# Windowed attention and an MoE-like mixer on one core: batch 0's score tiles and input, its mixing units in three banks, and a table of task ranks

## The chip, the cores and the metric

The kernel runs on one core of a Trainium2 chip, all eight batches one after the other. The metric is the device time of one execution in microseconds (us). The engines are PE (matrix products), PEld (PE's weight loads), DVE, ACT and POOL (elementwise work), and SP, on whose queue this kernel issues its loads and stores. Each engine works through its own instructions in the order in which the program lists them.

## The reference

```python
B, H, S, D = 8, 8, 576, 64
scores = q @ k.transpose(0, 1, 3, 2) / sqrt(D)
rel = pos[:, None] - pos[None, :]
mask_plain = (rel >= 0) & (rel < 32)                        # heads 0 to 3
mask_dil = (rel >= 0) & (rel < 128) & (rel % 4 == 0)        # heads 4 to 7
attn = softmax(where(mask, scores, -1e9))
x = (attn @ v).transpose(0, 2, 1, 3).reshape(B, S, 512)
theta = x @ w_theta                                         # 512 x 512
zr, zi = x * cos(theta), x * sin(theta)
y = einsum('ts,bsd->btd', w_tok_r, zr) + einsum('ts,bsd->btd', w_tok_i, zi)
u = x + y                                                   # w_tok: 576 x 576 each
out = u + relu(u @ w_ch)                                    # 512 x 512
```

q, k and v are float32; the weights arrive as 64-bit floats.

## The kernel before

**Attention.** Two heads make a pair, four pairs a batch. The sequence of a dilated head is permuted so that its window is 32 wide as well. A pair's 576 queries are 18 blocks of 32, and a block needs 64 keys. In `scores` one matmul serves one block of both heads: the queries stand as the 128 x 64 weight tile (two heads of 64 dims, and 64 columns, 32 for each head), with zeros where row and column belong to different heads, so that one product gives both heads' 32 rows of 64 scores. Two blocks fill the 128 partitions of one strip, nine strips a pair, in two PSUM banks of the pool `s`: strips 0 to 4 (20 PE instructions with the weight loads, as the trace counts them) and 5 to 8 (16). In batch 0 the mask is added by PE too (`mask_on_pe`): a matmul of the identity `ids` with the mask `mskb` opens each bank, and the scores add to it. Then come the maximum and the exponentials (line 626, three strips of 64 keys on ACT for each of the names P_0 to P_3), transposes, and `pv`, which gives x.

**Mixing.** All products of batch 0 behind theta are three products of split numbers: a high part (a cast to fp32r, `high`, line 455 on DVE or 458 on ACT) and a low part (the rest, `low`, line 463 on DVE or 466 on POOL). `theta0` makes theta of batch 0 for five tiles of the sequence (the last has 64 rows), `trig` its cosine and sine products, the nine tiles `z_0` to `z_8` with their low parts. A **unit** is one PSUM bank's worth of the work behind it: eight token units (`token`: 128 of the 512 features by half of the 576 positions, nine steps of three matmuls, 27 in all, one step for each z tile, in the order KORD), then eight channel units (`chan`, line 1453: four steps of three matmuls, one for each u tile). The first four token units use the first half of the token weights (`wt_g`, `wtkh`, `wtkl`), the other four the second half, `late_wt_a` and `late_wt_b`; the channel units use `late_wc`. These late tiles take the room of tiles of the attention of batch 0 and of the first weights.

**Weights.** `unpack` turns the 64-bit floats into float32: a load into a staging tile `st_...`, a clamp on DVE, an ACT step, a shift on DVE or ACT (the table SHIFT), and a merge on DVE (line 447); then the cast and the low part, each on an engine that small tables of keys choose (HIS, LOS, XLO, XEV, ZHI, ZLO, UHI, ULO). EARLY, LATE and LATE2 name the staging tiles; each load waits until its staging tile is free.

**The order.** `Order` is a list scheduler that runs while the program is built. Every part of the work is a generator that yields an engine and a cost in ns ahead of its instructions, or an event to wait for. Of the tasks that are ready on an engine it takes the one of lowest rank and writes its instructions down; the engines then run them in that order, and the tiles' semaphores keep the data right. RANK holds a number for each family of tasks; to it the program adds a step for each member (.01, or `pair` = 0.36 for the attention). All of batch 0, the attention and theta of batch 1 and the start of batch 2's scores are ordered in this way. From batch 1's first token unit on a planner with due times takes over (`steady`), one batch in 61.4 us.

The units of batch 0 are one task, one unit after the other, each in one of the two banks `m`:

```python
    def units(b):
        for f, i, g in UNITS:
            yield from f(b, i, g)
...
    go(units(0), RANK["units"])
```

and the scores, line 588 on, with `mask_on_pe` ahead of them:

```python
                for e in range(2):
                    qb = 2 * n + e
                    pe(nc.tensor.matmul(ps[64 * e:64 * e + 64, n - g0], q[:, qb],
                                        k[:, QB * qb:QB * qb + BW], start=not masked, stop=not masked or n == g1 - 1))
```

The functions that the change touches:

## Time and profile before

| | |
|---|---|
| three runs | 558.38, 558.6, 561.25 us; median 558.6 |
| profiled execution | 557.5 us, of which the span is 555.6 |
| mean granted PE clock | 0.991 |
| DMA | 124.42 MB, mean 224 GB/s |
| chain that ended last, by engine | PE 73%, ACT 8%, DMA 6%, DVE 5%, POOL 4% |

The span reaches from the first to the last instruction of the profiled execution; 1.9 us of it lie outside the span. Busy shares, windows and the rows of single stretches stand in the prediction. In those rows the columns are the start in us from the span's start, the duration, the engine, line, operation, the names `out<-in`, and how many instructions were merged (`x20`); brackets at the end give the engine's idle time ahead of it and what ended that. `128*64 128x64` on PE is a weight tile of 128 rows and 64 columns, and a result or operand of 128 x 64. A row of grouped instructions gives the busy time in us and the mean of one in ns. In a window's row stand PE, PEld, DVE, ACT and POOL busy, with the number of instructions in brackets, then the granted PE clock, the DMA engines' share, and GB/s.

### The profile page before, as it was taken

Reading aid. Unit: us, or ns where it says so; the run is one execution under the profiler, and the core shown is the slowest. Engines: PE = TensorE matmul, PEld = TensorE weight load, DVE = VectorE, ACT = ScalarE, POOL = GpSimd, SP = SyncE. Lnnn points to the kernel's source line nnn. Section 1 sums busy time; section 2 is a strip of 40 time slices with the busy share of each in tenths; the row PEclk is TensorE's granted clock in tenths of the full one; section 3 lists DMA queues with packets and bytes.
Section 4 is the critical chain, followed back from the end, with each engine's and each line's share of the span. In section 5 each row is a group of like instructions: output and inputs, shape, how many; then the busy total and the mean of one; then the engine's idle time right before and its main releaser. Section 6 shows DMA issues by size and latency. Waiting matters only on the chain.

```text
span 555.6 us, 14351 instructions
## 1 busy us (share of the span) xinstructions
PE 531.7 (96%) x5296; PEld 481.5 (87%) x5296; DVE 435.8 (78%) x1354; ACT 374.3 (67%) x1032; POOL 330.8 (60%) x349
## 2 busy tenths in 40 slices
PE   4899798999999999999999999999999999999997
PEld 3744687887898899998999899989999899989997
DVE  2878897995589697989799997989799988848422
ACT  1489977759938578668776777768775777467320
POOL 1227968799983274664477385656468365717660
PEclk9999799999999999999999999999999999999999
DMA  8993445644289947995489918994699826690722
GB/s 291 401 357 109 152 124 180 231 142 146 83 278 300 312 187 268 334 295 199 148 315 329 324 64 266 361 272 156 205 331 287 293 86 218 206 271 32 234 86 86
DMA packets 59127, 124.42 MB, mean 224 GB/s; under 512 B 5424, under 2 KB 24624, under 8 KB 58800
## 3 DMA queue, kind: packets, MB, share of 16 engines
q1 hardware_dynamic: 59056, 123.49, 64.9%
q8 instruction: 42, 0.69, 0.5%
q14 instruction: 29, 0.24, 0.1%
HBM read 99.88 MB, written 23.59 MB: 222 GB/s over the span
## 4 chain that ended last, share of the span: by engine, by line
PE 73%; ACT 8%; DMA 6%; DVE 5%; POOL 4%; issue 2%; SPq 0%; POOLq 0%; DVEq 0%; ACTq 0%
PE c L1453 15%; PE th L819 12%; PE C L1212 9%; PE D L1212 7%; PE A L1212 7%; PE o L750 6%; PE B L1212 4%; PE y L1420 4%; PE s L591 4%; DVE pt L650 2%; PE th L801 2%; DMA va<-in_vw_dram 2%; DMA st_wtk<-in_wtk_dram 1%; DMA q<-in_qT_dram 1%; ACT P L626 1%
## 5 line engine op out<-in xcount | busy, mean ns | idle before, releaser
L650 DVE STREAM_TRANSPOSE pt<-P 32x288 f32<-32x288 f32 x224 | 105.1, 469 | 11.3 <-POOL P L632 7.0
L1453 PE MATMUL c<-u,late_wc 128*128 128x288 f32 x768 | 109.1, 296 | 0.4 <-POOL late_wc L466 0.2
L1453 PEld LDWEIGHTS c<-u,late_wc 128*128 128x128 f32 x768 | 105.5, 188 | 4.0 <-DVE x L1429 0.7
L626 ACT ACTIVATE P<-P,mx 128x64 f32<-128x64 f32 x252 | 84.4, 337 | 3.0 <-DVE mx L530 2.9
L819 PE MATMUL th<-wthh,xh 128*128 128x512 f32 x224 | 75.0, 395 | 0.6 <-DVE K L1354 0.6
L632 POOL TENSOR_TENSOR P<-P,mx 128x576 f32<-128x576 f32 x32 | 38.7, 1210 | 59.9 <-DVE mx L630 51.6
L530 DVE CUSTOM_DVE_ANT_0 P<-s,mskb 128x64 f32<-128x64 f32 x252 | 39.0, 218 | 19.7 <-PE s L591 19.5
L1228 ACT CAST u<-x 128x288 fp32r<-128x288 f32 x48 | 20.6, 430 | 45.3 <-DVE x L1238 44.8
L819 PEld LDWEIGHTS th<-wthh,xh 128*128 128x128 f32 x224 | 42.0, 188 | 10.2 <-DVE K L1354 1.1
L1230 POOL TENSOR_TENSOR u<-x,u 128x288 fp32r<-128x288 f32 x48 | 41.7, 875 | 14.4 <-ACT u L1228 14.0
L626 ACT ACTIVATION_READ_ACCUMULATOR P<-P,mx 128x1 f32 x252 | 47.2, 187 | 0.0
L819 PE MATMUL th<-wthl,xh 128*128 128x512 f32 x112 | 44.4, 396 | 0.0
L710 ACT COPY x<-o 128x576 f32<-128x576 f32 x32 | 29.5, 921 | 20.0 <-PE o L750 20.0
L466 POOL TENSOR_TENSOR zl<-g,zh 128x512 fp32r<-128x512 f32 x7 | 9.1, 1299 | 49.3 <-ACT zh L458 49.3
L591 PE MATMUL s<-k,q 128*64 128x64 f32 x1008 | 37.0, 227 | 1.1 <-DVE K L1354 0.9
L591 PEld LDWEIGHTS s<-k,q 128*64 128x64 f32 x1008 | 33.1, 141 | 4.9 <-issue 2.3
L1429 DVE SCALAR_TENSOR_TENSOR x<-c,x 128x288 f32<-128x288 f32 x64 | 28.3, 449 | 11.6 <-PE c L1453 11.4
L750 PEld LDWEIGHTS o<-pt,va 128*64 128x64 f32 x600 | 20.3, 137 | 10.8 <-DVE pt L650 3.6
L750 PE MATMUL o<-pt,va 128*64 128x64 f32 x600 | 24.7, 227 | 4.9 <-DVE pt L650 3.3
L992 POOL TENSOR_TENSOR s<-f,x 128x256 f32<-128x256 f32 x24 | 17.8, 743 | 11.9 <-DVE f L980 9.7
L819 PEld LDWEIGHTS th<-wthl,xh 128*128 128x128 f32 x112 | 21.0, 188 | 4.1
L1420 PE MATMUL y<-wt_g,z 128*128 128x288 f32 x96 | 21.3, 327 | 3.4 <-POOL z L466 2.3
(245 smaller groups left out, 1583.7 us busy)
## 6 DMA issues: line engine op xcount, KB each, us to landing
q<-in_qT_dram SPq DMA_DIRECT2D x32, 576.0 KB, 5.5
late_wt_a<-tw_t SPq DMA_DIRECT2D x24, 576.0 KB, 6.2
wt_g<-tw_b SPq DMA_DIRECT2D x22, 576.0 KB, 6.4
va<-in_vw_dram SPq DMA_DIRECT2D x30, 320.0 KB, 5.2
k<-in_kT_dram SPq DMA_DIRECT2D x28, 304.0 KB, 5.6
out_dram<-x SPq DMA_DIRECT2D x28, 288.0 KB, 2.1
vb<-in_vw_dram SPq DMA_DIRECT2D x29, 256.0 KB, 4.3
xd<-xq SPq DMA_DIRECT2D x24, 288.0 KB, 4.9
```

Source lines behind the costliest of these rows:

```text
L530: pin(nc.vector.tensor_tensor_reduce(out=P[:, n], in0=ps[:, n - g0], in1=mskb[:, mask_of(pr, n)], op0=ALU.add, op1=ALU.min, scale=-SCALE, ...
L591: pe(nc.tensor.matmul(ps[64 * e:64 * e + 64, n - g0], q[:, qb], k[:, QB * qb:QB * qb + BW], start=not masked, stop=not masked or n == g1 - 1))
L626: table(nc.scalar.activation(P[:, n], P[:, n], AF.Exp, bias=mx[:, n:n + 1], scale=-1.0, accum_out=sm[:, n, :1]))
L632: pin(nc.gpsimd.tensor_tensor(P, P, mx.unsqueeze(2).to_broadcast([128, NJ, BW]), op=ALU.mult))
L650: pin(nc.vector.transpose(pmats[b, pr][k0:k0 + QB, :, hh, QB * e:QB * e + QB], P[p0:p0 + QB, :, QB * o:QB * o + QB]))
L710: pin(nc.scalar.copy(dst, src))
L750: pe(nc.tensor.matmul(ps[64 * hh:64 * hh + 64, BW * j:BW * j + BW], v[:, 64 * hh:64 * hh + 64], pmats[b, pr][:, j, hh], start=True, stop=T ...
L819: pe(nc.tensor.matmul(pt, l, r, start=(n == 0), stop=(n == 3 * NC - 1)))
L1212: pe(nc.tensor.matmul(ps, l, r, start=first and n == 1, stop=last and n == 3 * len(ks), skip_group_check=more))
L1230: pin(nc.gpsimd.tensor_tensor(ul[b, d][:, ts], x[:, ts], uh[b, d][:, ts].bitcast(F32), op=ALU.subtract))
L1420: pe(nc.tensor.matmul(ps, l[:, cs], r, start=(n == 0), stop=(n == 3 * NK - 1)))
L1453: pe(nc.tensor.matmul(ps, l[:, cs], r[:, ts], start=(n == 0), stop=(n == 3 * NC - 1)))
```

## The change

It has four parts.

1. **Scores of batch 0.** Its queries come as an input of their own, `q0`, without the zeros: 128 x 576 for a pair, 288 KB in place of 576 KB. A block of 32 queries is two matmuls now, one for each head, with 64 rows and 32 columns of weights, so a pair has 72 of the PE instructions where it had 36. They open the bank, and the mask is added behind them and closes it. The loads of the mask and the identity move behind the queries and keys of the first pair on SP's queue. Batches 1 to 7 keep their form.
2. **Units of batch 0.** Each of the 16 units is a task with a rank. Unit n waits for the end of unit n - 3 (LANES), so three are open at a time; U0 gives them banks of the pools t, x and s as well as m, and token units go through the z tiles in the order KORD0.
3. **Ranks.** RANK has a number for each task: each pair, each weight tile, each theta tile, each unit. Turns (the flips of batch 1 and 2), evacuations and the trig work of each theta tile have their own.
4. **Engines and rooms.** The tables that choose DVE, ACT or POOL for casts, low parts and shifts are different, the staging tiles EARLY, the banks of theta and x in batch 1 (TP1, XN1), and two delays (AT1 12 to 10, SLACK 500 to 0).

The diff, cut:

```diff
-EARLY = ('u0', 'u1', 'u2', 'u3', 'xh0')
+EARLY = ('xh2', 'u2', 'u1', 'u3', 'xh1')
...
-RANK = dict(load=6.64, scores0=1.09, flip=0.01, pv0=1.13, pair=0.36, theta_unpack=1.54, theta0=5.3, trig0=2.031, token_early=4.156, theta_split=6.42, token_late=5.835, chan=2.1, units=2.95, evacuate=4.49, scores1=4.02, scores2=7.3, pv1=8.0, theta1=5.96, trig1=8.298)
-SHIFT = (('wth', 0), ('wth', 2), ('wtk0_', 0), ('wtk0_', 2), ('wtk0_', 4))
+RANK = dict(
...
+    units=(1.534, 1.575, 1.534, 1.534, 1.534, 1.534, 1.534, 4.786, 4.642, 6.706, 1.534, 4.702, 4.682, 4.692, 4.672, 4.712),
...
+SHIFT = (('wth', 0), ('wth', 2), ('wth', 3), ('wtk0_', 2), ('wtk0_', 4))
...
-LOS = ()
-XLO = (0, 1, 2)
-XEV = ()
-ZHI = ((0, 8),)
-ZLO = ((1, 6),)
-UHI = ((1, 2, 0),)
-ULO = ((1, 3, 0),)
+LOS = (('wch', 3), ('wth', 1), ('wtk', 1, 4))
+XLO = (2,)
+XEV = ((0, 3),)
+ZHI = ((0, 8), (1, 0), (1, 2), (1, 4))
+ZLO = ((1, 1), (1, 3))
+UHI = ((1, 1, 0), (1, 2, 0), (1, 2, 1), (1, 3, 0), (1, 3, 1))
+ULO = ((0, 1, 1), (1, 0, 0), (1, 0, 1), (1, 2, 1), (1, 3, 1))
...
+KORD0 = (0, 4, 1, 5, 7, 2, 6, 8, 3)
+LANES = 3
...
-TP1 = {4: 't', 0: 't', 1: 't', 2: 't', 3: 't'}
+TP1 = {4: 't', 0: 't', 1: 't', 2: 's', 3: 'x'}
...
-XN1 = {4: 'x', 0: 's', 1: 'x', 2: 'm', 3: 'x'}
+XN1 = {4: 's', 0: 's', 1: 's', 2: 'm', 3: 'x'}
...
-U0 = 'mmmmmmmmmmmmmmmm'
+U0 = 'mmtmmtmmxmmmmsmm'
...
     def first_loads():
-        yield "DMA", dma(3 * BW + 64)
-        pin(nc.sync.dma_start(mskb, maskb.bitcast(BF16)))
-        pin(nc.sync.dma_start(idb, identb.bitcast(BF16)))
         for pr in range(NP):
...
-            yield "DMA", dma(2 * S)
-            pin(nc.sync.dma_start(q, qT[0, pr]))
+            yield "DMA", dma(S)
+            pin(nc.sync.dma_start(q, q0[pr]))
...
             if pr == 0:
+                yield "DMA", dma(3 * BW + 64)
+                pin(nc.sync.dma_start(mskb, maskb.bitcast(BF16)))
+                pin(nc.sync.dma_start(idb, identb.bitcast(BF16)))
...
-                                start=(n == g0), stop=False))
+                                start=False, stop=(e == g1)))
...
-                    pe(nc.tensor.matmul(ps[64 * e:64 * e + 64, n - g0], q[:, qb],
-                                        k[:, QB * qb:QB * qb + BW], start=not masked, stop=not masked or n == g1 - 1))
+                    if b:
+                        pe(nc.tensor.matmul(ps[64 * e:64 * e + 64, n - g0], q[:, qb],
+                                            k[:, QB * qb:QB * qb + BW], start=True, stop=True))
+                        continue
+                    for hh in range(2):
+                        hs, to = slice(64 * hh, 64 * hh + 64), 64 * e + QB * hh
+                        pe(nc.tensor.matmul(ps[to:to + QB, n - g0], q[hs, qb], k[hs, QB * qb:QB * qb + BW],
+                                            start=(n == g0), stop=False))
...
-    def units(b):
-        for f, i, g in UNITS:
-            yield from f(b, i, g)
+    def unit(n):
+        if n >= LANES:
+            f, i, g = UNITS[n - LANES]
+            yield None, ("tk" if f is token else "ch", 0, i, g)
+        f, i, g = UNITS[n]
+        yield from f(0, i, g)
...
     def thetas(b):
-        for st in STS:
+        for n, st in enumerate(STS):
+            yield "rank", RANK["theta1"][n]
             yield from theta(b, st)
-            go(trig(b, st), RANK["trig1"])
+            go(trig(b, st), RANK["trig1"][STS.index(st)])
...
-    go(units(0), RANK["units"])
+    for n in range(len(UNITS)):
+        go(unit(n), RANK["units"][n])
```

What this does to the order is shown at three places. In the rows, `x10` counts neighbours that read alike.

The first is PE at the start of the program: the scores of pair 0 (banks `s_0_0` and `s_0_5`), the mask through the identity (`ids`), and the queries `q_0`. Before:

```order
L545 LDWEIGHTS ids
L545 MATMUL s_0_0_126<-mskb,ids 128x64
L545 LDWEIGHTS ids
L545 MATMUL s_0_0_126<-mskb,ids 128x256
L591 MATMUL s_0_0_126<-first_k,q_0_110 64x64 x10
L545 LDWEIGHTS ids
L545 MATMUL s_0_5_143<-mskb,ids 128x256
L591 MATMUL s_0_5_143<-first_k,q_0_110 64x64 x8
```

The same place after:

```order
L617 MATMUL s_0_0_126<-first_k,q_0_101 32x64 x20
L568 LDWEIGHTS ids
L568 MATMUL s_0_0_126<-mskb,ids 128x64
L568 LDWEIGHTS ids
L568 MATMUL s_0_0_126<-mskb,ids 128x256
L617 MATMUL s_0_5_157<-first_k,q_0_101 32x64 x16
L568 LDWEIGHTS ids
L568 MATMUL s_0_5_157<-mskb,ids 128x256
```

The scores stand ahead of the mask, as twice as many matmuls of half the rows.

The second is PE where the first token units of batch 0 begin: `y_0_0`, `y_1_0`, `y_2_0` are the units for the features 0 to 127, 128 to 255 and 256 to 383, `th_3` is the last theta tile, `z_0` and `z_4` are the first trig products, `s_0_5` and `s_1_0` scores of batch 1. Before:

```order
L1420 MATMUL y_0_0_647<-wt_g,z_0_618 128x288 x3
L801 MATMUL th_3_559<-st_wth_103,x_3_480 128x512
L1420 MATMUL y_0_0_647<-wtkh_544,z_4_570 128x288
L1420 MATMUL y_0_0_647<-wtkl_545,z_4_570 128x288
L1420 MATMUL y_0_0_647<-wtkh_544,z_4_570 128x288
L591 MATMUL s_0_5_685<-k_0_105,q_0_104 64x64 x8
L591 MATMUL s_1_0_701<-k_1_575,q_1_574 64x64 x10
```

The same place after:

```order
L1450 MATMUL y_2_0_733<-wt_g,z_0_691 128x288 x3
L830 MATMUL th_3_634<-st_wth_105,x_3_557 128x512
L1450 MATMUL y_0_0_707<-wtkh_715,z_4_647 128x288
L1450 MATMUL y_0_0_707<-wtkl_716,z_4_647 128x288
L1450 MATMUL y_0_0_707<-wtkh_715,z_4_647 128x288
L1450 MATMUL y_2_0_733<-wtkh_715,z_4_647 128x288
L1450 MATMUL y_2_0_733<-wtkl_716,z_4_647 128x288
L1450 MATMUL y_2_0_733<-wtkh_715,z_4_647 128x288
L1450 MATMUL y_1_0_764<-wt_g,z_0_691 128x288 x3
L1450 MATMUL y_1_0_764<-wtkh_715,z_4_647 128x288
L1450 MATMUL y_1_0_764<-wtkl_716,z_4_647 128x288
L1450 MATMUL y_1_0_764<-wtkh_715,z_4_647 128x288
```

Each z tile is used by three units as soon as it stands in the order, where one unit used it and the next came back to it later.

The third is ACT around the casts of the second half of the token weights, `late_wt_b`: `P_2` and `P_3` are the exponentials of batch 1, `x_0` its copy of a result, `u_3` a cast of batch 0, `st_wch` a step of the channel weights. Before:

```order
L710 COPY x_0_899<-o_0_900 128x576
L626 ACTIVATE P_2_901,sums_96<-P_2_901,mx_2_902 128x64 x3
L458 CAST late_wt_b<-st_wtk_2_414 128x576
L626 ACTIVATE P_2_901,sums_96<-P_2_901,mx_2_902 128x64 x3
L458 CAST late_wt_b<-st_wtk_3_483 128x576
L626 ACTIVATE P_2_901,sums_96<-P_2_901,mx_2_902 128x64 x3
L626 ACTIVATE P_3_970,sums_97<-P_3_970,mx_3_971 128x64 x3
L458 CAST late_wt_b<-st_wtk_4_740 128x288
L626 ACTIVATE P_3_970,sums_97<-P_3_970,mx_3_971 128x64 x3
L458 CAST u_3_1092<-x_3_480 128x288
```

The same place after:

```order
L739 COPY x_0_1018<-o_0_1019 128x576
L481 CAST u_3_1007<-x_3_557 128x288
L481 CAST late_wt_b<-st_wtk_2_614 128x576
L655 ACTIVATE P_2_1020,sums_96<-P_2_1020,mx_2_1021 128x64 x9
L655 ACTIVATE P_3_1081,sums_97<-P_3_1081,mx_3_1082 128x64 x3
L481 CAST late_wt_b<-st_wtk_3_560 128x576
L655 ACTIVATE P_3_1081,sums_97<-P_3_1081,mx_3_1082 128x64 x3
L462 ACTIVATE st_wch_1134<-st_wch_1134 128x512
L655 ACTIVATE P_3_1081,sums_97<-P_3_1081,mx_3_1082 128x64 x3
L468 ACTIVATE st_wch_1134<-st_wch_1134 128x512
L481 CAST late_wt_b<-st_wtk_4_349 128x288
```

The first cast stands ahead of the exponentials of `P_2` and behind a cast of u; the second has come behind all of `P_2`.

Two more things in words. In PE's order of before, 16 of the 32 steps of batch 0's channel units stand ahead of the first theta tile of batch 1, and 16 between theta and the scores that follow; of after, 23 stand ahead and 9 behind. From the first token unit of batch 1 on, PE's order is the same to the end.

More of the change, by code (lines that the diff above doesn't have):

```diff
@@ L68 @@
 GATE = ()
-AT1, AT2 = 12, 14
+AT1 = 10
+AT2 = 14
 FIRST = 2
@@ L189 @@
 TABLE = 1280.0
-SLACK = 500.0
+SLACK = 0
 LATENCY = dict(PE=100.0, DVE=100.0, ACT=130.0, POOL=130.0, DMA=1800.0)
@@ L602, in scores @@
             give("qk", rqk)
-            go(load_qk(b * NP + pr + 2), RANK["load"])
+            go(load_qk(b * NP + pr + 2), RANK["load"][0])
         if b and on_pe(b, pr):
@@ L756, in pv @@
             give("va", ra)
-            go(load_va(n + 2), RANK["load"])
+            go(load_va(n + 2), RANK["load"][0])
         if rb is not None:
             give("vb", rb)
-            go(load_vb(NP if n == NP - 2 else n + 1), RANK["load"])
+            go(load_vb(NP if n == NP - 2 else n + 1), RANK["load"][0])
         if b:
@@ L803, in theta0 @@
             signal(("th0", st, c))
-        go(trig(0, st), RANK["trig0"] + .01 * STS.index(st))
+        go(trig(0, st), RANK["trig0"][STS.index(st)])
     def theta(b, st):
@@ L1406, in token @@
     def token(b, d, g):
-        yield None, ("z", b, KORD[0])
-        yield None, ("wtk", g, KORD[0] // 2)
+        order = KORD if b else KORD0
+        yield None, ("z", b, order[0])
+        yield None, ("wtk", g, order[0] // 2)
         ps, rel = yield from bank(unit_bank(b, NC * g + d), f"y{b}_{d}_{g}")
@@ L1412, in token @@
         n = 0
-        for kt in KORD:
+        for kt in order:
             yield None, ("z", b, kt)
```

74 lines of the change are left out of this document (47 added, 27 removed).

## The prediction

> **What bounds the kernel now.** I read the page first, then the chain that ended last in order of time, then busy time by windows, then the timeline of the windows that differ.
>
> ```profile
> span 555.6 us, 14351 instructions
> PE 531.7 (96%) x5296; PEld 481.5 (87%) x5296; DVE 435.8 (78%) x1354; ACT 374.3 (67%) x1032; POOL 330.8 (60%) x349
> 200.50 7.98 PE c L1453 x60
> 261.92 7.98 PE c L1453 x60
> ```
>
> The columns of the chain are start, duration, what. PE is idle for 555.6 - 531.7 = 23.9 us in all. The two `c` pieces end two neighbouring batches and lie 61.42 us apart: from batch 2 on a batch is PE work in an unbroken row, and nothing there is touched. The windows (PE, PEld, DVE, ACT, POOL busy, granted clock, DMA share, GB/s) show where the idle time is.
>
> ```profile
> 0.00:10.00 10.00, 3.54 (x41) 2.48 (x41) 1.71 (x9) 1.28 (x1) 2.26 (x6) 1.00 0.73 241
> 10.00:20.00 10.00, 8.89 (x171) 7.80 (x173) 6.27 (x17) 2.15 (x4) 1.58 (x2) 1.00 1.03 409
> 20.00:30.00 10.00, 8.34 (x202) 6.60 (x198) 8.96 (x22) 6.80 (x12) 3.29 (x3) 1.00 1.04 397
> 40.00:50.00 10.00, 9.45 (x48) 4.59 (x46) 8.28 (x12) 9.97 (x17) 6.47 (x5) 1.00 0.18 46
> 50.00:60.00 10.00, 7.92 (x74) 5.02 (x73) 10.00 (x42) 9.99 (x20) 9.62 (x8) 0.91 0.58 216
> 60.00:70.00 10.00, 8.04 (x41) 7.58 (x41) 8.56 (x23) 9.99 (x43) 8.41 (x8) 0.75 0.35 120
> 70.00:80.00 10.00, 9.82 (x138) 8.86 (x136) 9.58 (x36) 6.81 (x17) 6.87 (x6) 1.00 0.26 69
> 90.00:100.00 10.00, 7.28 (x84) 6.31 (x84) 8.71 (x27) 6.41 (x11) 7.34 (x8) 0.83 0.37 136
> sum 200.00, PE 179.55 PEld 149.68 DVE 154.73 ACT 140.26 POOL 125.48; mean PE 8.98 PEld 7.48 DVE 7.74 ACT 7.01 POOL 6.27
> ```
>
> Of the 23.9 us, 200 - 179.55 = 20.45 lie in the first 200 us. Three stretches stand out: the opening, where the DMA engines are full (share 1.03 and 1.04) and PE waits for loads; 40 to 70, where ACT is busy 29.95 of 30 us and PE idles while its granted clock falls to 0.75; and 90 to 100. The change acts on all three. Its last place is the first token of batch 1:
>
> ```profile
> 142.06 0.67 PE L1420 MATMUL y<-wt_g,z 128*128 128x288 f32 x3
> 146.36 0.40 PE L1420 MATMUL y<-wt_g,z 128*128 128x288 f32 x1 [1.19 <-POOL z L466]
> ```
>
> From the row at 142.06 on, PE's order is the same in both programs to the last instruction, and the other engines' orders join a little later. So the question is how much earlier that row comes; the rest, 413 us, moves with it.
>
> **The opening.** The first score waits for its key load.
>
> ```profile
> 6.66 1.33 PE L591 MATMUL s<-first_k,q 128*64 128x64 f32 x20 [3.21 <-DMA first_k<-in_kT_dram]
> 8.25 1.12 PE L591 MATMUL s<-first_k,q 128*64 128x64 f32 x16
> 16.84 0.92 PE L686 MATMUL pT<-ids,P 64*64 64x64 f32 x20
> 18.56 0.80 PE L591 MATMUL s<-first_k,q 128*64 128x64 f32 x20
> 20.78 0.80 PE L686 MATMUL pT<-ids,P 64*64 64x64 f32 x20 [0.36 <-POOL P L632]
> q<-in_qT_dram SPq DMA_DIRECT2D x32, 576.0 KB, 5.5
> first_k<-in_kT_dram SPq DMA_DIRECT2D x4, 304.0 KB, 7.8
> mskb<-in_maskb_dram SPq DMA_DIRECT2D x1, 96.0 KB, 2.0
> ids<-in_identb_dram SPq DMA_DIRECT2D x1, 32.0 KB, 1.8
> ```
>
> Ahead of that score stood 96 + 32 + 576 + 304 = 1008 KB; now 288 + 304 = 592 KB. The 416 KB (0.43 MB) less, at the 241 GB/s of the first window, are 1.8 us. Over four pairs the queue carries 4 x 288 KB = 1.18 MB less, 2.9 us at 409 GB/s, for all that is loaded behind; the better bound of the opening is a gain of 2.9.
>
> Against it stands the score form. A pair was 36 PE instructions in 1.33 + 1.12 = 2.45 us; it becomes 72. No row shows a 64x32 tile. From below: four tiles overlap so well that the 72 take the old 2.45 (less than that has no reason, since the same keys stream). From above: each costs the old 66 ns (1.33/20), 4.8 us, so 2.3 more per pair and 9.4 for four. The nearest row is pT, a 64x64 tile, at 46 ns (0.92/20): 72 of them are 3.3 us, 0.85 more per pair, 3.4 for four. I take that. The cover is PE's own idle time from 10 to 30 us, 1.11 + 1.66 = 2.8, and the 1.8 us of earlier start, 4.6 together; without it the 3.4 would be added whole. So theta of batch 0 moves **1.2 us** earlier (4.6 - 3.4); bounds: 2.9 earlier, 9.4 - 4.6 = 4.8 later. That the mask and identity loads move behind the first pair on SP's queue costs nothing here: 128 KB are 0.5 us, less than the scores they now follow.
>
> The rule that speaks against this form is in the Trainium skill, page TensorEngine Tiling (Array Packing), section Restrictions and Gotchas: different row tiles cannot access one PSUM bank at the same time, and each new pair of half-heads is two row tiles in one bank. The trace does not bear it out: the two row tiles of pT share a bank too, and 20 of them took 0.80 us at 20.78, as long as 20 full-height scores at 18.56.
>
> **Three units in three banks.** The z tiles come from a queue on ACT that has no gap.
>
> ```profile
> 38.73 0.59 ACT L1352 ACTIVATE Kg<-th 64x512 int32<-64x512 f32 x1
> 62.70 0.61 ACT L458 CAST z<-K 128x512 fp32r<-128x512 f32 x1
> 49.60 0.66 ACT L458 CAST wthh<-st_wth 128x512 fp32r<-128x512 f32 x1
> 64.80 0.50 PE L1420 MATMUL y<-wt_g,z 128*128 128x288 f32 x1 [0.90 <-POOL z L466]
> 149.81 3.79 PE y L1420 x27
> ```
>
> From the first trig instruction to the last z cast ACT takes 62.70 - 38.73 = 24 us. The new order has the same pieces there less one weight cast (0.66). So the last z comes 1.2 + 0.7 = 1.9 us earlier and no more. What changes is PE's stock of work: a unit is 27 matmuls, 3.79 us, and nine steps. When the last z arrived, PE had done six of the nine steps of one unit; in the new order it has done eight of two units and three of a third, 19 against 6, so 13 x 3.79 / 9 = **5.5 us** is done ahead. With the 1.9 that is 7.4, what PE had idle from 50 to 70 (2.08 + 1.96) and lost to the clock there (0.9 + 2.5), so it just fits. This stock is worth something only if the late weights come earlier too.
>
> ```profile
> 80.39 0.73 ACT L458 CAST late_wt_b<-st_wtk 128x576 fp32r<-128x576 f32 x1 [0.67 <-DVE st_wtk L447]
> 81.20 3.48 POOL L466 TENSOR_TENSOR late_wt_b<-st_wtk,late_wt_b 128x576 fp32r<-128x576 f32 x2 [2.58 <-ACT late_wt_b L458]
> 85.03 0.56 PE L1420 MATMUL y<-late_wt_b,z 128*128 128x288 f32 x3
> L626 ACT ACTIVATE P<-P,mx 128x64 f32<-128x64 f32 x252 | 84.4, 337 | 3.0 <-DVE mx L530 2.9
> ```
>
> PE first needs `late_wt_b` at 85.03 and has no wait there: PE itself is late. In the new order its stock makes it early, and the cast with the low part behind it (3.48/2 = 1.74 us) is the bound. Ahead of the cast ACT has three exponentials less (1.0 us) and one u cast more (about 0.4); DVE has some 1.5 us more (the x copy and a low part that ACT and POOL gave up), for which its idle time from 60 to 80 is the cover (1.44 + 0.42 = 1.9 us). I put the cast 1.2 + 0.6 = 1.8 earlier, at 78.6, and the low part's end at 78.6 + 0.73 + 1.74 = 81.1. So PE gets there 3.9 us earlier, having done two steps more (0.8): **4.7 us** ahead. Were DVE's cover gone, the cast would stay where it is, and 2.9 would be left.
>
> **To theta of batch 1.** Now the channel weights are last.
>
> ```profile
> 94.93 0.74 PE L750 MATMUL o<-pt,va 128*64 128x64 f32 x17 [2.72 <-DVE pt L650]
> 98.16 0.33 SPq L430 DMA_DIRECT2D st_wch<-in_wch_dram  x1
> 110.60 1.75 POOL L466 TENSOR_TENSOR late_wc<-st_wch,late_wc 128x512 fp32r<-128x512 f32 x1
> 112.41 5.36 PE L1453 MATMUL c<-u,late_wc 128*128 128x288 f32 x37 [0.21 <-POOL late_wc L466]
> 117.61 0.39 PE L824 MATMUL th<-wthh,xh 128*128 128x512 f32 x1
> 127.33 0.49 PE L819 MATMUL th<-wthh,xh 128*128 128x512 f32 x1 [0.42 <-DVE K L1354]
> 131.06 0.69 DVE L1354 SCALAR_TENSOR_TENSOR K<-th,K 128x512 f32<-128x512 f32 x1 [0.39 <-ACT K L1352]
> ```
>
> The wait of 2.72 at 94.93 is for the transposes of P_2; in the new order DVE puts P_3's sums between them, so I leave it a wait of about 1. The fourth channel load waited at 98.16 for a staging tile that the second weight's low part frees, and its own chain took 112.4 - 98.2 = 14.2 us. The chain keeps its staging tiles, and the load is still behind q_2 on SP's queue. I expect the tile 2 us earlier, at 96, and the chain in 11.3 us (its last low part is a DVE subtraction now, near the 0.69 of 131.06, in place of 1.75 on POOL, and its pieces have first rank; the rest of the 2.9 is an estimate): 107.3, 5.1 us earlier. Then 14 of the steps c are left before theta, of 0.4 us (7.98/60 x 3): theta at 112.9, 4.7 earlier than 117.6, with 7 steps c fewer behind it (2.8): 7.5. The bounds: the chain comes with the 1.2 of the opening alone, 1.2 + 2.8 = 4.0; or it keeps up with PE's stock, about 10.
>
> **The last stretch gives some back.** The steps c covered theta's waits for its bank. With them gone, the third theta tile waits for a copy on ACT (0.59, as at 38.73) and a subtraction on DVE (0.69) with one set of transposes as cover, and theta's trig work reaches the last z with less PE time ahead of the stall at 146.36. I take 1.0 us for each, 2.0; bounds 0.5, about what the wait at 127.33 is now, and 4, where each of four theta tiles waits 1.0. Sum: 7.5 - 2.0 = **5.5 us**.
>
> Behind 142 the queues hold what they held: ACT has 198 rows ahead of batch 1's last z cast for 202 before. The span becomes 555.6 - 5.5 = 550.1, and with the 1.9 us around it (557.5 - 555.6) the execution 552.0. The median of the runs shown, 558.6, lies 1.1 above the profiled 557.5; I add half of that: **552.5**.
>
> **The rivals.**
> - *The queues eat it.* ACT and DVE are full from 40 to 80, and every earlier piece needs a gap in them. If cast and channel chain come no earlier than the opening, 4.0 at theta less 2.0 is 2.0: 556.0, within 0.5%. For it: 29.95 of 30 busy. Against it: from 90 on ACT is busy 6.41 of 10.
> - *Row tiles exclude one another.* By the skill's rule the halves of a pair run one after the other. At the 66 ns of row 6.66 the opening loses 4.8 where I count a gain of 1.2: 6.0 less, 558.5, the same. Slower begins at 77 ns each: 5.5 us per pair, 3.1 more than now, 4 x 3.1 - 4.6 = 7.8 later, 9.0 behind the forecast, 561.5. A tile alone, without its neighbour, would be 2 x 66 = 132 ns: 9.5 us per pair, 28 more in all, some 577. For it only the rule; against it pT's rows.
> - *The tail.* If theta's waits cost the full 4 and the channel chain brings nothing, 4.0 - 4 = 0, 558: the same.
> - *Better.* If PE's stock runs through, 10 less 0.5 is 9.5, 548.5. The clock speaks for it: 0.91, 0.75 and 0.83 of three windows are 5.1 us of full clock lost, which my sum doesn't give back.
>
> That the units do not interleave is no rival: the order shows them do it.
>
> **How the numbers follow.** Forecast (549.5 to 555.5) 0.64; better 0.10; queues 0.11; tail 0.04; row tiles at 66 ns 0.05, and from 77 ns on 0.06. A measurement of this kernel tells about 0.5%, 2.8 us, from no change, so faster means below 555.8 here: 0.64 + 0.10 and a little of the queues, 0.76. Slower, above 561.4: 0.06 and some of the tail, 0.08. Same: 0.16. The range takes in better and the same: 547 to 559; only the slower case and the edges are left out.
>
> **What would show it.** First score near 4.9 us; 20-step score groups at 40 instructions in about 1.8 us (2.7 would be the rival). Last z cast of batch 0 near 60.8. `late_wt_b` first used near 81, with PE waiting for it. A wait for `late_wc` near 107. First token of batch 1 near 136.5. I am wrong in the mechanism if PE is not ahead at the last z, or if the score groups in the opening are what PE waits for; wrong in size if the late weights or the channel chain come at the old times.

## The result and the profile after

The changed kernel takes **562.22 us** (median of 20 runs, 560.2 to 577.88) where the kernel before takes 558.0 in the same comparisons (20 runs, 554.93 to 561.25): a ratio of **1.0074, 95% interval 1.0056 to 1.0093**, slower by 0.7%. The single run at 577.88 was a disturbed one and is not in the ratio. The forecast was 552.5, faster. The profiled execution took 561.54, with a span of 559.7; 4.1 more than before's span. From the page of the kernel after:

```profile
span 559.7 us, 14648 instructions
PE 529.9 (95%) x5440; PEld 480.3 (86%) x5440; DVE 440.8 (79%) x1366; ACT 371.5 (66%) x1024; POOL 328.9 (59%) x345
```

PE is idle for 559.7 - 529.9 = 29.8 us, 5.9 more than before. The windows of the kernel after, six of those in the prediction and three more at the end that turn out to matter (the sum is that of all twenty windows from 0 to 200):

```profile
0.00:10.00 10.00, 4.91 (x150) 3.58 (x150) 3.17 (x11) 1.97 (x2) 2.25 (x6) 1.00 0.82 260
10.00:20.00 10.00, 6.94 (x196) 5.81 (x196) 6.12 (x18) 2.15 (x4) 2.30 (x2) 0.83 1.03 406
20.00:30.00 10.00, 9.22 (x188) 6.39 (x188) 8.62 (x20) 7.07 (x13) 2.32 (x2) 1.00 0.57 192
50.00:60.00 10.00, 7.99 (x84) 6.00 (x84) 9.96 (x32) 9.96 (x18) 10.00 (x8) 1.00 0.33 96
60.00:70.00 10.00, 9.61 (x71) 9.37 (x71) 6.19 (x22) 9.98 (x44) 6.85 (x6) 1.00 0.43 145
70.00:80.00 10.00, 8.10 (x103) 6.96 (x103) 9.65 (x29) 6.34 (x13) 7.49 (x7) 0.83 0.16 44
130.00:140.00 10.00, 7.99 (x39) 6.29 (x37) 7.26 (x10) 8.16 (x16) 9.61 (x10) 1.00 0.18 63
140.00:150.00 10.00, 9.98 (x144) 9.46 (x145) 6.85 (x38) 9.11 (x29) 10.00 (x11) 0.83 0.06 15
170.00:180.00 10.00, 7.74 (x88) 7.64 (x89) 6.74 (x30) 6.41 (x26) 3.46 (x4) 0.83 0.90 291
sum 200.00, PE 173.97 PEld 145.38 DVE 156.86 ACT 135.25 POOL 121.14; mean PE 8.70 PEld 7.27 DVE 7.84 ACT 6.76 POOL 6.06
```

The stretch that the stock of units was to fill is better: from 50 to 70 PE idles 2.01 + 0.39 = 2.4 us where it idled 4.04, and its clock there is full. From 90 to 100 PE is busy 7.78 us at full clock where it was busy 7.28 at 0.83. But PE idles more in 10 to 20, in 130 to 140 and in 170 to 180, and the lowered clock (0.83 over ten us) stands in new places. Cut at the program's own marks (theta of batch 0, the end of the first half of the units, theta of batch 1, the first token of batch 1, the long row of `c` behind batch 1's token units), the windows of the kernel after are:

```profile
0.00:25.88 25.88, 16.96 (x492) 13.79 (x492) 13.86 (x38) 7.49 (x12) 5.71 (x9) 0.93 0.82 298
25.88:63.62 37.74, 35.55 (x290) 20.83 (x289) 34.34 (x89) 33.49 (x63) 22.63 (x16) 1.00 0.71 238
63.62:116.55 52.93, 46.11 (x527) 42.66 (x526) 42.71 (x149) 41.51 (x146) 40.28 (x39) 0.97 0.52 176
116.55:142.44 25.89, 21.53 (x142) 17.60 (x140) 21.90 (x40) 17.96 (x32) 22.47 (x24) 0.97 0.30 107
142.44:204.50 62.06, 58.32 (x567) 54.47 (x566) 48.21 (x166) 38.38 (x120) 34.03 (x40) 0.96 0.75 250
```

and of the kernel before:

```profile
0.00:27.73 27.73, 18.51 (x384) 15.78 (x385) 15.12 (x43) 8.20 (x14) 6.36 (x10) 1.00 0.92 346
27.73:63.62 35.89, 32.20 (x231) 16.87 (x227) 31.05 (x82) 33.46 (x62) 21.26 (x17) 0.95 0.66 238
63.62:117.61 53.99, 49.40 (x534) 45.50 (x534) 46.51 (x156) 41.25 (x146) 41.14 (x40) 0.94 0.51 169
117.61:142.06 24.45, 23.74 (x162) 20.01 (x160) 16.78 (x31) 18.32 (x32) 22.85 (x25) 1.00 0.28 97
142.06:200.50 58.44, 56.20 (x566) 51.92 (x563) 45.77 (x157) 39.52 (x124) 34.38 (x41) 1.00 0.81 270
```

PE's idle time (length less the first figure behind it) in the five stretches is 8.9, 2.2, 6.8, 4.4 and 3.7 us after, 9.2, 3.7, 4.6, 0.7 and 2.2 before. So the first two stretches gain, and the last three give it all back: theta of batch 1 is 1.06 earlier, the first token 0.38 later, and the row of `c` 3.5 later (204.01 for 200.50 on the chain that ended last; the cut at 204.50 lies half a us inside the row). Each mark is that of one execution. The changed kernel and the runs vb_act and bank_t below have the same order up to theta of batch 1, and show it at 116.55, 117.19 and 118.99, so a difference of an us at theta is no more than the scatter. Three questions for the experiments: why the opening gains so little, why the work done ahead at theta is worth nothing at the first token, and why over three more us are lost behind it, in a part that the change was not to touch.

### The profile page after: what moved, and what is told of

The parts are those of the page before. It is cut to its first block, busy times and chain, and to the rows that moved or that the text cites. A ratio compares the mean times of both kernels' runs of the same rounds, so it can differ in the third digit from the quotient of the medians.

```text
span 559.7 us, 14648 instructions
## 1 busy us (share of the span) xinstructions
PE 529.9 (95%) x5440; PEld 480.3 (86%) x5440; DVE 440.8 (79%) x1366; ACT 371.5 (66%) x1024; POOL 328.9 (59%) x345
## 4 chain that ended last, share of the span: by engine, by line
PE 71%; DVE 10%; DMA 7%; ACT 7%; POOL 2%; issue 2%; SPq 1%; POOLq 0%; DVEq 0%; ACTq 0%
PE c L1483 14%; PE th L848 11%; PE C L1241 8%; PE A L1241 7%; PE D L1241 6%; PE o L779 5%; PE y L1450 5%; PE s L612 4%; PE B L1241 4%; DVE pt L679 3%; DMA st_wch<-in_wch_dram 2%; PE th L830 2%; DMA q<-in_qT_dram 1%; DMA xn<-xd 1%; ACT P L655 1%
## 5 line engine op out<-in xcount | busy, mean ns | idle before, releaser
L661 POOL TENSOR_TENSOR P<-P,mx 128x576 f32<-128x576 f32 x32 | 36.9, 1154 | 66.8 <-DVE mx L659 61.0
L553 DVE CUSTOM_DVE_ANT_0 P<-s,mskb 128x64 f32<-128x64 f32 x252 | 39.0, 217 | 17.7 <-PE s L612 17.5
L739 ACT COPY x<-o 128x576 f32<-128x576 f32 x31 | 28.3, 914 | 28.8 <-PE o L779 28.7
L989 ACT ACTIVATE cos<-f,halfpi 128x512 f32<-128x512 f32 (+1 forms) x30 | 20.7, 689 | 4.4 <-DVE g L928 3.1
```

The source lines that it names most:

```text
L553: pin(nc.vector.tensor_tensor_reduce(out=P[:, n], in0=ps[:, n - g0], in1=mskb[:, mask_of(pr, n)], op0=ALU.add, op1=ALU.min, scale=-SCALE, ...
L661: pin(nc.gpsimd.tensor_tensor(P, P, mx.unsqueeze(2).to_broadcast([128, NJ, BW]), op=ALU.mult))
L739: pin(nc.scalar.copy(dst, src))
```

## The experiments

Each run is one kernel. Where a table of ranks or the form of the scores is edited, the scheduler writes a new order for everything; where "the order is kept", the order of all instructions was written in from the kernel named, so that only the edit differs. "First o" is the start of the first row `o` of batch 1's token stretch (the end of its first token unit), and "theta to z" the time from theta of batch 1 to the end of its last z low part. Before has 147.49 and 28.69 for them, after 147.10 and 29.20.

### The score form, alone and taken back

**scores_only** is the kernel before with part 1 alone, newly ordered; **no_scores** the kernel after without part 1, newly ordered.

> The kernel before with part 1 alone: batch 0's own queries, scores from 64x32 tiles, the mask behind them; units, ranks and engine tables as before. Theory A (the opening spends its earlier start itself, on PE waits that the profile puts down to issue, and on half clock): first score near 4.7 us, one or two issue waits of 1 to 2 us before 25 us, first trig instruction on ACT (Kg) within 0.5 us of the 38.7 of before, 557 to 559.5 us, ratio to before 0.998 to 1.003. Rival (the earlier start comes through as forecast): first trig near 37.5, 556 to 557. Rival (the form itself costs): score groups of 40 over 1.8 us at full clock, over 560.

> The changed kernel with part 1 taken back (zero-padded queries, 64x64 tiles, mask first); lanes, ranks and tables stay. Theory A: no issue wait over 0.5 us before 25 us, first trig instruction at 38 to 40, the waits behind 60 us stay as kinds, 560 to 564 us: part 1 is not what makes the change slower. Rival (part 1 is the loss): 558 or less.

Measured: scores_only 570.11 us, ratio 1.0215 (1.0177 to 1.0253); no_scores 575.53, ratio 1.0303 (1.0257 to 1.035). Both miss by far, since the scheduler re-ordered what lies behind: PE waits 5.46 us for an ACT copy of x and 4.61 for a cast of late_wc in the one, 5.06 for a cast of `wtkh` and 7.69 for a DVE subtraction in the other. They say nothing of part 1 by itself. What they do show is in their first 30 us: scores_only has waits of 0.38, 0.74 and 1.56 that end with "issue", no_scores has none.

So the same two edits with the orders kept. **form_alone** is before's order with the new form and the 288 KB loads; **form_back** is after's order with the old form and the 576 KB loads (the mask still behind the first pair's loads).

```diff
-                    for hh in range(2):
-                        hs, to = slice(64 * hh, 64 * hh + 64), 64 * e + QB * hh
-                        pe(nc.tensor.matmul(ps[to:to + QB, n - g0], q[hs, qb], ...
+                    pe(nc.tensor.matmul(ps[64 * e:64 * e + 64, n - g0], q[:, qb], ...
```

> The kernel before in its own order, with only the form of batch 0's scores and its query loads changed: 64x32 tiles, 72 instructions a pair, 288 KB, the mask's matmuls behind the scores; the mask's loads stay first on SP's queue. Theory A: first score near 5 us, issue waits of 1 to 3 us in all before 28 us, first trig instruction at 38 to 39.3, 557 to 559.5 us. Rival (the forecast's opening): first trig at 37.5 or earlier, 557 or less.

> The changed kernel in its own order, instruction for instruction, with only the tile form of batch 0's scores and its loads taken back: 64x64 tiles, 36 instructions a pair, queries of 576 KB with their zeros; the mask stays behind them. Theory A (part 1 brings nothing behind the opening): first score about 2 us later, the issue waits before 25 us gone, first trig instruction within 0.7 us of 37.9, 561 to 563.5 us. Rival (part 1 is worth the forecast's 1.2 us and more): over 563.5. Rival (part 1 is what loses): under 560.5.

Measured: form_alone **561.48**, ratio 1.0061 (1.0036 to 1.0086), where less was expected; form_back 561.95, ratio 1.0061 (1.0034 to 1.0087), in its total as expected. Part 1 alone costs 0.6% in before's order, some 3.4 us of the median (the profiled execution, 559.37, is one of the fastest; its end is 2.0 later than before's), and taking it out of after's order brings nothing that can be told (1.0061 against 1.0074). A cause is visible on PE's timeline of form_alone:

```profile
13.00 0.55 PE L596 MATMUL s<-first_k,q 64*32 64x64 f32 x25
14.88 0.31 PE L596 MATMUL s<-first_k,q 64*32 64x64 f32 x7 [1.33 <-issue]
21.17 0.33 PE L757 MATMUL o<-pt,first_v 128*64 128x64 f32 x2 [2.42 <-issue]
27.39 0.80 PE L693 MATMUL pT<-ids,P 64*64 64x64 f32 x19 [1.82 <-issue]
```

A bank's row of 32 scores stops after 25 and goes on 1.33 us later, and the profile names nothing that it waited for ("issue"). Counted from the start, PE has done 220, 346 and 473 matmuls at the three stops. In the kernel after:

```profile
4.67 1.29 PE L617 MATMUL s<-first_k,q 64*32 64x64 f32 x40 [4.67 <-DMA first_k<-in_kT_dram]
10.60 0.76 PE L617 MATMUL s<-first_k,q 64*32 64x64 f32 x40 [0.99 <-DVE mx L658]
11.71 0.55 PE L617 MATMUL s<-first_k,q 64*32 64x64 f32 x25
13.95 0.31 PE L617 MATMUL s<-first_k,q 64*32 64x64 f32 x7 [1.69 <-issue]
20.27 0.33 PE L779 MATMUL o<-pt,first_v 128*64 128x64 f32 x2 [0.95 <-issue]
25.88 1.76 PE L830 MATMUL th<-st_wth,x 128*128 128x512 f32 x3
```

Here too the stops come at matmul 220 and 346. The page's queues and one half us of the DMA view, both of the kernel after, name what is late:

```profile
q8 instruction: 43, 0.70, 0.5%
```

```profile
q8 instruction: 1, 0.02, 12.1%
```

One queue carries PE's instructions: 43 transfers of 0.70 MB / 43 = 16 KB. In the kernel after they land at 11.0 to 11.5, 17.5 to 18 and 22 to 22.5 us, and the stops end at 13.95 and 20.27, some 2 to 3 us behind a landing. In form_alone they land at 12.5 to 13, 18.5 to 19 and 24.5 to 25, and the stops end at 14.88, 21.17 and 27.39. In before they land at 17.5 to 18 and 24 to 24.5: PE reached its matmul 212 only at 20 us (41 + 171, the windows in the prediction), and never had to wait. The share of the DMA engines is 1.03 in that window. So the opening has a second supply that can run out: with 144 matmuls more, and as many weight loads, PE reaches the end of a block before the next one is there. The number of instructions is not all of it. form_back has the old form in after's order, and it was expected to be free of these waits; its PE is through 218 matmuls at 17.3 us, before only at some 20, and stops as well, though its block lands at 16.5 to 17:

```profile
19.23 0.33 PE L777 MATMUL o<-pt,first_v 128*64 128x64 f32 x2 [1.93 <-issue]
```

How long a stop lasts varies between executions of one order: 1.69 and 0.95 in after, a single one of 1.08 in vb_act. The Trainium skill, page Runtime: NRT & Kernel Launch, section Instruction fetch mechanics, says that an engine fetches its instructions by its own DMA queue in blocks of 16 KiB, 256 instructions, at a cost that is mostly hidden. The block fits the trace (126 and 127 matmuls with their weight loads between the stops are 252 and 254 instructions, and 43 blocks of 256 are 11,008, for 10,880 matmuls and weight loads in all); "hidden" does not hold here: 1.33 + 2.42 + 1.82 = 5.57 us in form_alone. That the instruction blocks wait behind the loads is an inference from the landing times and the full engines; a run with the same instructions and fewer bytes was not made.

### The stock of units

**lanes1** is the kernel after with one unit at a time in one pool of banks.

```diff
-LANES = 3
+LANES = 1
-U0 = 'mmtmmtmmxmmmmsmm'
+U0 = 'mmmmmmmmmmmmmmmm'
```

> The changed kernel with one unit at a time (LANES 1, all units in the banks m as before); ranks per task, score form and tables stay. PE's order then has 5 steps c ahead of the first theta tile of batch 1, where the changed kernel has 23. Theory B (from theta's first tile to batch 1's first token the chain of trig work on ACT and DVE takes about 24.5 us whatever PE has done ahead, so a stock of work on PE is worth nothing): first theta tile 2 to 4 us earlier than 116.6, first token of batch 1 at 139 to 143, 559 to 563 us in all. Rival (the stock is what PE lives on, as forecast): without it first token 4 to 6 us later than 142.4, 566 us or more.

Measured: 565.51, ratio 1.014 (1.0101 to 1.0179): theta of batch 1 at 119.59, the first token at 150.34, PE waits of 1.89, 1.40 and 0.96 for late_wt_b. The theory expected theta 2 to 4 us earlier than after and missed it by far; its rival, that PE lives on the stock, is nearly met. The stock is worth having: without it the first token comes 7.9 us later than after.

### The late weights

The merge of the first tile of `late_wt_b` stands on DVE behind the transposes of batch 1's first two pairs. **merge_first** puts these pairs behind it.

```diff
-    turn1=(3.477, 3.484, 3.365, 3.51),
+    turn1=(5.859, 5.859, 3.365, 3.51),
```

> The changed kernel with the ranks of batch 1's first two turns raised from 3.477 and 3.484 to 5.859, so that on DVE the merge of the first late_wt_b tile (st_wtk 2) stands behind 4 of the 16 transposes of those pairs and not behind all; the schedule around it moves along, and all 32 steps c now stand ahead of theta's first tile. Theory D (the first cast of late_wt_b, at 80.4 in both kernels, is set by that place on DVE): the cast comes at 73 to 77. For the whole time it says little, since theta starts behind 9 more steps c: 559 to 566 us. Rival (the cast is set by ACT's own queue, as the forecast had it): it stays at 79.5 to 81.

Measured: 567.81, ratio 1.0191 (1.0134 to 1.0248), a little above the 559 to 566 expected. DVE and ACT of the kernel after, ACT of merge_first:

```profile
71.20 5.82 DVE L679 STREAM_TRANSPOSE pt<-P 32x288 f32<-32x288 f32 x12
79.62 0.75 DVE L470 SCALAR_TENSOR_TENSOR st_wtk<-st_wtk 128x576 uint32<-128x576 uint32 x1
```

```profile
62.57 0.61 ACT L481 CAST z<-K 128x512 fp32r<-128x512 f32 x1
80.41 0.72 ACT L481 CAST late_wt_b<-st_wtk 128x576 fp32r<-128x576 f32 x1 [0.18 <-DVE st_wtk L470]
```

```profile
76.53 0.70 ACT L481 CAST late_wt_b<-st_wtk 128x576 fp32r<-128x576 f32 x1
```

The cast comes 3.9 us earlier, as expected, so the place in DVE's queue did hold it. But the pairs that were put back are then late themselves: all 32 steps `c` run ahead of theta, which comes at 125.70. The transposes have to be done somewhere.

### The last stretch before the first token

**tail_vb** keeps the edit of vb_act (below) and gives four of the channel units higher ranks, so that fewer steps `c` stand ahead of theta of batch 1 and more behind it.

```diff
-    units=(..., 4.702, 4.682, 4.692, 4.672, 4.712),
+    units=(..., 4.702, 6.682, 6.692, 6.672, 6.712),
```

> The run with vb on ACT's queue, and the ranks of the last four channel units of batch 0 raised from about 4.7 to 6.7: 18 steps c stand ahead of the first theta tile of batch 1 where the changed kernel has 23, and 14 behind it. Theory B (the trig chain that starts with that theta tile sets the first token of batch 1, so steps c done ahead of it only delay it): first theta tile near 114.5 in place of 116.6, first token at 140 to 141.5 in place of 142.4, 1 to 2.5 us less than the run with vb on ACT's queue alone, so 555 to 557.5. Rival (theta's inputs are not ready earlier, or the waits inside theta grow by as much): the same as that run within 0.7 us.

Measured: 562.75, ratio 1.009 (1.0062 to 1.0117), where 555 to 557.5 was expected. Theta comes at 114.44, 2.1 earlier than after; the first token at 147.55, 5.1 later. Next to vb_act, of which it is an edit, theta is 2.75 earlier, the first o 3.45 later and the whole slower. PE has its cover of steps `c` and waits all the same, here on PE's timeline of tail_vb:

```profile
129.64 0.50 PE L848 MATMUL th<-wthh,xh 128*128 128x512 f32 x1 [3.60 <-DVE K L1383]
```

The first reading of theta's bank on DVE starts at 121.56 there (120.37 after), behind transposes and copies. That reading is 7.1 us behind theta, where in after it is 3.8. Theta to z is 34.49. This points to the trig work on ACT and DVE, more than to PE's work, as what spans this stretch: over before, after, vb_act, form_back, form_alone, bank_t and trig_tail theta to z lies between 28.69 and 29.50, though PE has 16 to 23 steps `c` done at theta in them. But these are few different orders, and in six other kernels, with other orders of DVE or POOL, it is 30.5 to 34.5.

**bank_t** (vb_act with the last xn of batch 1 in another bank, order kept) asks whether the wait of 2.03 us for that bank matters. **trig_first** puts batch 2's first two pairs behind batch 1's trig work on DVE as well, and **trig_tail** adds the ranks of tail_vb to that.

```diff
-XN1 = {4: 's', 0: 's', 1: 's', 2: 'm', 3: 'x'}
+XN1 = {4: 's', 0: 's', 1: 's', 2: 'm', 3: 't'}
...
-    turn2=(7.357, 7.784),
+    turn2=(8.95, 8.96),
```

> The run with vb on ACT's queue, and one PSUM bank changed: batch 1's last set of transposes (xn of theta tile 3) goes to bank t in place of bank x, which theta tile 3 itself holds. All orders stay as they are. Theory B (the chain of trig work sets the first unit's end, not PE): the wait of 2.0 us ahead of those transposes goes, PE waits for the last z in its place, the last z is ready at 146.7 as before within 0.5, the first output product of batch 2 (o) starts within 0.5 of 147.9, 558.5 to 560.5 us. Rival (PE's waits in the tail are what the change lost): o 1.5 to 2 us earlier, 557.8 or less.

> As the run with the bank changed, and the transposes of batch 2's first two pairs get a rank behind batch 1's trig work (turn2 8.95, 8.96 in place of 7.357, 7.784). PE's order stays, word for word; on DVE some of the transposes stand behind the first subtractions of the trig chain. Theory D (DVE's transposes, which stand ahead of the chain's first steps, lengthen it): from theta's first tile to the last z 27.5 to 28.7 us in place of 29.5, o 1 to 2 us earlier than in the run with the bank changed, 557 to 559. Rival (the chain is ACT's, and the transposes are then late for o): no gain, 559 or more.

> As the run before, and with the ranks of the last four channel units raised as in the tail run: fewer steps c ahead of theta's first tile. Theory D: first theta tile near 114.5, 28 to 29.5 us from it to the last z (34.5 in the tail run), o at 144 to 145.5, 555 to 557.5 us, as fast as the kernel before or faster. Rival (the chain grows by as much as it starts earlier, as in the tail run): 560 or more.

Measured: bank_t 560.1, ratio 1.0032 (1.0012 to 1.0052): the wait of 2.03 is gone, and waits of 0.81 and 1.35 for z stand in its place; theta to z is 29.18, and theta to the first o 29.95 for 30.70 in vb_act, a gain of 0.75 at most. trig_first 561.82, ratio 1.0071 (1.0039 to 1.0104): no gain where 557 to 559 was expected, theta to z 30.51. trig_tail 559.85, ratio 1.0033 (1.0011 to 1.0056): here theta comes at 114.80, theta to z is 29.02, and the first o comes at 144.61, 2.9 us earlier than before, as expected. trig_tail and trig_first differ in the ranks of four units alone, and here fewer steps `c` ahead of theta go with a theta 2.4 (as much as the mark scatters) and a first o 4.3 earlier: the opposite of tail_vb against vb_act. The total was expected at 555 to 557.5 and is not there: loads for the attention of the batches behind are late now, on PE's timeline of trig_tail:

```profile
167.76 0.69 PE L779 MATMUL o<-pt,vb 128*64 128x64 f32 x16 [1.71 <-DMA vb<-in_vw_dram]
169.09 1.27 PE L612 MATMUL s<-k,q 128*64 128x64 f32 x36 [0.65 <-DMA k<-in_kT_dram]
```

Two more waits, 0.60 at 204.94 and 0.93 at 211.94, are for a DVE result x. A lead of 2.9 us at the first o has become 556.4 - 555.6 = 0.8 us behind at the end of the profiled run.

### Behind the first token

The last loss of the kernel after, PE and the chain that ended last:

```profile
172.26 1.12 PE L779 MATMUL o<-pt,vb 128*64 128x64 f32 x16 [3.74 <-DMA vb<-in_vw_dram]
173.17 2.11 PE L612 MATMUL s<-k,q 128*64 128x64 f32 x36
```

```profile
159.92 7.10 DMA q<-in_qT_dram
167.09 5.13 DMA vb<-in_vw_dram
```

The same place before:

```profile
170.03 0.69 PE L750 MATMUL o<-pt,vb 128*64 128x64 f32 x16 [0.30 <-DMA vb<-in_vw_dram]
```

```profile
166.54 3.45 DMA vb<-in_vw_dram
```

PE of the kernel after is there at 172.26 - 3.74 = 168.52, 1.2 us earlier than before (169.73). The load of vb leaves SP 0.55 us later, behind stores `tw_t` and behind a load of q that takes 7.10 us to land, and takes 1.68 longer itself. 1.2 + 0.55 + 1.68 are 3.4 of the 3.74, and the 0.30 that was waited for before makes 3.7. While it was in flight the DMA engines were fuller than before: a share of 0.91 and 296 GB/s from 167.09 to 172.22, for 0.73 and 216 GB/s from 166.54 to 169.99. Behind the wait the same 36 scores take 2.11 us, not 1.22 as before: PE runs at half its clock for a while (0.83 in 170 to 180, where before had 1.00). The two rows of `o` and scores end up 175.21 - 172.26 = 2.95 us long where they were 1.67, so the half clock costs 1.28 here.

**vb_act** keeps the order and issues this one load from ACT's queue. **st_pool** issues the stores `tw_t` from POOL's queue.

```diff
-        pin(nc.sync.dma_start(vb, vw[b, pr, :, VA:]))
+        pin((nc.scalar if (b, pr) == (2, 3) else nc.sync).dma_start(vb, vw[b, pr, :, VA:]))
```

> The changed kernel with one load moved: vb of batch 2's fourth pair, the one that PE waits 3.7 us for at 168.5, is issued from ACT's queue in place of SP's. Every engine's order is the same but for this one instruction. Theory C (that wait comes from SP's queue: behind stores of weight sums and behind the landing of a 576 KB load): the load is issued near 164 in place of 167.1, the wait falls under 1 us, the half clock behind it goes, 557 to 559 us, ratio to before 0.997 to 1.003. Rival (the DMA engines are full, whoever issues): it lands near 172 as well, 561 us or more.

> The changed kernel with the stores of the weight sums (tw_t) issued from POOL's queue in place of SP's; PE's order is the same. Theory C (batch 1's load of vb for the fourth pair is late because SP's queue holds it behind those stores and a 576 KB load behind them): the PE wait of 3.7 us at 168.5 falls to under 0.7 us, the granted clock from 170 to 180 goes back to 1.00, 556.5 to 558.5 us. Rival (the DMA engines are full there, whoever issues): a wait of over 2 us stays, 560 to 562.5.

Measured: vb_act **559.68**, ratio 1.0032 (1.0002 to 1.0061). PE and its window in vb_act:

```profile
170.35 0.69 PE L779 MATMUL o<-pt,vb 128*64 128x64 f32 x16 [1.03 <-DMA vb<-in_vw_dram]
```

```profile
170.00:180.00 10.00, 9.19 (x107) 9.01 (x108) 7.51 (x36) 7.22 (x32) 3.45 (x4) 1.00 0.94 300
```

One DMA on another queue takes 2.5 us off the median of after (2.3 by the ratios, whose intervals just overlap), and the half clock behind that wait is gone with it; the load left ACT's queue at 163.87 and took 6.4 us to land. A wait of 1.03 and 559.68 just miss what was expected. The queue is not all of the cause: with the load on ACT's queue the wait is 0.31 in tail_vb, 1.58 in bank_t and 1.71 in trig_tail, but 2.93 in trig_first, where it leaves at 167.40. st_pool took 571.23 where 556.5 to 558.5 was expected, ratio 1.0237 (1.0198 to 1.0276): the wait for vb is gone there too, but the stores now stand in the queue of the engine that makes z low parts, theta to z is 33.55, and PE waits 4.31 for one xn.

None of the twelve runs is faster than the kernel before. The best of the changed order, vb_act, bank_t and trig_tail, are 0.3% slower than it.

## Why the prediction was wrong, step by step

- **First score near 4.9.** Right, 4.67. **The form at 46 ns a tile.** Too dear: 40 of the new PE instructions take 0.76 us at full clock, 19 ns each, so a pair's 72 take no longer than its 36 did. The rival of the excluded row tiles is refuted. For this form the trace does not agree with the rule of the Trainium skill, page TensorEngine Tiling (Array Packing), section Restrictions and Gotchas, that different row tiles cannot access one bank at the same time: 20 full-height scores take 0.80 us. The rows of pT in the prediction could not speak against it, since their 20 took as long as 20 full-height ones and so show no overlap.
- **Theta of batch 0 moves 1.2 us earlier.** By its number right (25.88 for 27.73, 1.85 earlier), but two things stand against each other in it, so the number is partly luck: cheaper tiles, and 1.69 + 0.95 us of waiting for instructions that the sum did not know. And it was no measure of progress: in the new order a part of pair 3's transposes and sums stands behind theta's start.
- **The last z comes 1.9 earlier, at 60.8.** Failed: 62.57 for 62.70. The first trig instruction was where it had been (37.89 and 38.94 in the two tiles that PE feeds first, 38.73 before), and ACT's row of work behind it is as long.
- **PE has 19 steps done when the last z arrives.** Right in kind: PE's idle time from 50 to 70 fell from 4.04 to 2.40, and lanes1 shows what is lost without it.
- **The cast of late_wt_b at 78.6.** Failed: 80.41 for 80.39. I read the cast as ACT's matter with DVE's cover behind it; the row that I quoted ended its wait with the merge on DVE, and that merge stands behind all transposes of two pairs (79.62 for 79.60; merge_first moves it). I gave the case "DVE's cover gone" 2.9 of the 4.7 and did not take it. PE is 2.2 ahead at its first late_wt_b (82.81 for 85.03), where I had 3.9.
- **Theta of batch 1 at 112.9, and seven steps fewer behind it: 7.5.** This is the step that failed most ahead of the first token: theta came at 116.55. The seven steps are there: 69 matmuls `c` ahead of theta, 23 steps, for 16 before, 2.8 us. The channel weights were no bound either; the first `c` comes at 97.81, for 109.78. But theta moved only 1.06, since PE waits between 63.6 and 116.6 for late_wt_a, late_wt_b, the transposes and a row of scores, 6.8 us in all for 4.6; rows of them in the kernel after, and one of DVE:

```profile
74.13 0.53 PE L1450 MATMUL y<-late_wt_a,z 128*128 128x288 f32 x2 [1.12 <-POOL late_wt_a L489]
92.89 0.74 PE L779 MATMUL o<-pt,va 128*64 128x64 f32 x17 [1.44 <-DVE pt L679]
95.84 0.40 PE L1450 MATMUL y<-late_wt_b,zh 128*128 128x288 f32 x1 [0.79 <-DVE late_wt_b L486]
107.34 0.80 PE L612 MATMUL s<-k,q 128*64 128x64 f32 x20 [1.61 <-issue]
105.18 1.34 DVE L460 TENSOR_SCALAR st_wch<-st_wch 128x512 f32<-128x512 f32 x1 [1.29 <-DMA st_wch<-in_wch_dram]
```

  The wait of 1.61 ends with "issue", but no instruction block lands near it, and the key of these scores had landed at 105.8 (100.67 + 5.1). In all seven runs that have this wait, PE's weight load goes on 0.08 us behind DVE's fifth reading of the bank of scores ahead of them (its end is at 107.23 here), and these readings stand behind the clamp of a channel weight, which waited 1.29 us for its load. So it is most likely that clamp, put early by its new rank, that holds the scores; no run moved it.

  And the 2.8 did not come through to the first token. In after, as in before, the last z comes some 29 us behind theta. Whether a step `c` ahead of theta then delays the first token by its 0.4 us, so that I counted as won what the trig work waits for, is argued and not shown: trig_tail against trig_first speaks for it, tail_vb against vb_act and lanes1 speak against it.
- **The last stretch gives back 2.0.** Mis-sized: of the 3.9 us that PE was ahead at theta (1.06 + 2.8) nothing was left at the first token (142.44 for 142.06), 4.2 lost. PE's waits in it are on DVE's trig work:

```profile
128.45 0.50 PE L848 MATMUL th<-wthh,xh 128*128 128x512 f32 x1 [1.62 <-DVE K L1383]
140.02 0.66 PE L939 MATMUL xn<-ids,x 128*128 128x128 f32 x4 [2.03 <-DVE K L1383]
142.44 1.09 PE L1450 MATMUL y<-wt_g,z 128*128 128x288 f32 x3
147.10 0.62 PE L779 MATMUL o<-pt,va 128*64 128x64 f32 x13
```

  The wait of 1.19 at 146.36 is gone in exchange, so that at the end of the first unit the new order is 0.39 ahead. The wait of 2.03 and the half clock behind it seem to set that end, since the last z was ready at 145.75; but bank_t, without that wait, gains 0.75 at most.
- **"The rest, 413 us, moves with it."** This is the step that made the forecast wrong in sign. It rested on PE's order being the same from there on, which it is; but SP's order is not, nor is what the DMA engines carry. From the first o to the end before takes 408.1 us and after 412.6: 4.5 us, of which 0.39 + 2.23 are the later vb (170.03 to 172.26) and 1.28 the half clock behind it; the last 0.6 comes later and was not followed. vb_act, where one load is moved, takes 409.7 for that part, and 2.5 less in the median. The case was not among my rivals.
- **The clock as a reason for "better".** The half clock did leave 50 to 70 and 90 to 100, but it came back elsewhere: 0.83 in 10 to 20, 70 to 80, 140 to 150 and 170 to 180, 1.7 us of full clock each, for 0.91, 0.75 and 0.83 before. Not all of that is time lost, since PE waits in a part of it: in 170 to 180 the matmuls took 1.28 us longer.

In all: some 3.9 us of PE's work done ahead at theta were worth 0.4 at the first o, and became a loss of 4.1 by a load behind it and the clock that falls with the wait. Two steps failed. The stretch up to the first token did not move by 5.5 us, since PE's waits for late weights, transposes and scores ahead of theta, and for DVE's trig work behind it, took what the stock had won. And the rest did not move with it: 412.6 us in place of 408.1. The second is supported by vb_act to some 2.3 to 2.5 us. For the first the waits are seen, but what sets the time from theta to the first token stays open, and the opening's waits, the late weights and the wait for vb that stays were not taken apart. Open stays, too, why the load of vb takes 5.13 us for 3.45: the DMA engines were fuller during it, and no run emptied them there. In trig_tail the lead at the first o is lost to two loads and to DVE; no run had both a lead there and its loads in time.

## What to carry to other kernels

Work done ahead is a gain only where the end waits for that work; ask first which chain sets the end. Here the stock on PE was needed (lanes1), and the 2.8 us of it that stood ahead of theta were still worth nothing at the first token, where PE waited for DVE. "The order of the bound engine is the same from here on" is not "the time is": compare the queue that issues its loads too, and find the load that came only just in time before (PE waited 0.30 us for it). And an edit that adds instructions to a stretch where the DMA engines are full, or lets PE through it sooner, should be priced in instructions too, not in their durations alone.
